# Linear attention with a mixture of experts on one core: one copy of the second layer's code per step, and evictions in one ScalarE operation

## The chip, the cores and the metric

The kernel runs on 1 core of one Trainium2 chip. The metric is the device time of the whole program in microseconds (us), the median of several runs. Engines are written as in the profile: PE is TensorE, DVE is VectorE, ACT is ScalarE, POOL is GpSimd, SP is SyncE. Each engine has its own instruction stream; a suffix q in a row (PEldq, ACTq) marks what its sequencer does: waits, branches, issues.

## What is computed

The reference is attention with positive random features, followed by a mixture of experts in which every token goes to one expert:

```python
def phi(x):                                   # x = q or k, scaled
    h = einsum('bhsd,md->bhsm', x, omega) - sum(x * x, -1, keepdims=True) / 2
    return exp(h - max(h, -1, keepdims=True)) / sqrt(m)
kv, z = einsum('bhsm,bhsd->bhmd', k_p, v), sum(k_p, axis=2)
attn = einsum('bhsm,bhmd->bhsd', q_p, kv) / (einsum('bhsm,bhm->bhs', q_p, z)[..., None] + 1e-6)

logits = x @ w_gate                           # x: 4608 tokens of 512
expert_idx = argmax(logits, axis=1)
gate_w = softmax(logits)[arange(N), expert_idx]
for e in range(8):
    mask = expert_idx == e
    out[mask] = gate_w[mask, None] * (maximum(x[mask] @ w1[e], 0) @ w2[e])
```

There are 8 batches of 8 heads with 576 positions of 64, 128 features, and 8 experts with `w1` of 512 x 1024 and `w2` of 1024 x 512. All of it is float32.

## The kernel before

The first part (class `Attention`, to about 250 us) computes the attention of all batches and writes its rows to a buffer in HBM, `token_rows`; `Routing` sorts the tokens by expert meanwhile. The second part (class `Experts`) goes over the experts in steps. A step takes up to three tiles of 128 tokens of one expert: it gathers their rows by index (POOL), turns and splits them into a high and a low part (`xh`, `xl`, on ACT and DVE), multiplies them with the expert's first layer (`l1`, L1031: three products for each pair of blocks, high by high, high by low, low by high), takes the relu into `hh` and `hl` (ACT at L1045, DVE at L1046), multiplies with the second layer (`l2`, L1072 to L1074, again three products), scales the result by the token's gate and scatters it to the output (`send` and `scatter`).

How many tokens an expert has is known only on the chip. The steps are written out in the program one after the other, and each holds the code of all its kinds: two tiles (kind 2, 256 columns in the first layer), two tiles and a half one (kind 1, 320 columns) and three tiles (kind 0, 384 columns). Each engine loads the kind into a register (L960) and branches. In `l1` this happens twice per step, once for each half of the hidden units (`part`): `If(kind > 1)` at L1059, and in its `Else` `If(kind > 0)` at L1062, so that the code of a part is, in this order, that of two tiles, of the half tile and of three tiles. The second layer is `l2(t, a)` for tile a, with 24 products of 512 columns; a half third tile has a routine of its own, `l2half`, with 16.

With this input 15 steps run, numbered here from 1: steps 4, 9 and 14 are of kind 0, steps 5, 11 and 15 of kind 1, the other nine of kind 2. From step 13 on the steps are nested in one another (`tail`), with a branch at L1166 that leaves when no step is left.

The order within an engine is that of the program. In `step`, the engines run the splits of the weights that have arrived (`change`, casts at L54 and subtractions at L48), the first layer, the gathers of step t + 2, the turning and splitting of the rows of step t + 1 (`following`), and then the second layer with its evictions and scatters. The part that the change touches is the end of `step`: `If(kind > 1)` at L1148 holds the two tiles of a two-tile step, the second of them under a flag of its own (`when`, L1111); its `Else` holds the third tile first (the branch between `l2half` and `l2(t, 2)` is at L1152) and then tiles 0 and 1 once more. Each `l2` accumulates in a PSUM bank of its own (`p_2[a]`: `p_t`, `p_snu`, `p_skv`) and ends in `send`, which evicts the bank in two halves of 256 columns: ACT takes the first (L1101), DVE the second (L1102), and POOL scatters the row tile (L1106). Both halves write one tile `y`, and DVE's half starts after ACT's.

Of the kernel before, what the change touches and what calls it, by code (L numbers as in the profile page):

```python
# [14 lines left out]
AF = mybir.ActivationFunctionType  # L15
# [6 lines left out]
DM = H * D  # L22
# [823 lines left out]
class Experts:  # L846
# [121 lines left out]
    def split(self, n, cs=range(8)):  # L968
        for c in cs:
            split_r(self.nc, *self.part(n, c), self.nc.scalar, self.nc.vector)  # L970
# [126 lines left out]
        self.send(p, self.ys[i % 3], self.gt[i % 6], idx[:, i:i + 1])  # L1097

    def send(self, p, y, gate, idx):
        c = DM // 2  # L1100
        self.nc.scalar.activation(y[:, :c], p[:, :c], AF.Copy, scale=gate)  # L1101
        self.nc.vector.tensor_scalar_mul(y[:, c:], p[:, c:], gate)  # L1102
        self.scatter(y, idx)

    def scatter(self, y, idx):
# [27 lines left out]
    def step(self, t, following, split=lambda: None):  # L1133
        engines = (ET.PE, ET.DVE, ET.Activation, ET.Pool)
        if t + 1 < NPR:
            self.flips(t + 1)
            self.flips3(t + 1)
        split()
        kind = self.kind(t, engines)
        self.l1(t, kind)  # L1140
        if t + 2 < NPR:
            self.gather(t + 2)
            self.gather3(t + 2)
        if t == 1:
            self.next(0, 2)
        following()
        self.nc.gpsimd.drain()
        with self.tc.If(kind > 1) as pair:  # L1148
            self.l2(t, 0)
            self.when(self.reg(4, t, 1, engines), lambda: self.l2(t, 1))  # L1150
        with pair.Else():
            with self.tc.If(kind > 0) as short:  # L1152
                self.l2half(t)
            with short.Else():
                self.l2(t, 2)
            for a in range(2):
                self.l2(t, a)

    def tail(self, t):
        split = lambda: self.change(t, 2)  # L1160
# [103 lines left out]
```

## Time and profile before

| what | us |
|---|---|
| median of 3 runs | 676.98 (676.61 to 679.22) |
| the profiled execution, its own time | 676.33 |
| its span, from the first to the last recorded instruction | 674.6 |
| PE busy in the span | 639.4 (95%) |
| ACT, DVE, POOL busy | 417.1, 346.1, 281.8 |
| DMA queue q8 (code) | 92 packets, 1.51 MB |

The profile records one execution. Its span is a little shorter than the time that the execution took, and the sum of a prediction is made against the latter. A row of a view that groups instructions has the line of the kernel, the engine, the operation, the tiles written and read, the shape, and a count; what stands behind the bar is the time busy, the mean of one in ns, and the idle time of the engine before them with what ended it. What ended a wait is inferred from semaphores: where the engine that is named had long been done, it was something else. Branches and register loads are not counted as busy time; they appear where one line is asked for, with shortest, median and longest duration in ns.

### The profile page before, as it was taken

Reading aid. Unit: us, or ns where it says so; the run is one execution under the profiler, and the core shown is the slowest. Engines: PE = TensorE matmul, PEld = TensorE weight load, DVE = VectorE, ACT = ScalarE, POOL = GpSimd, SP = SyncE. Lnnn points to the kernel's source line nnn. Section 1 sums busy time; section 2 is a strip of 40 time slices with the busy share of each in tenths; the row PEclk is TensorE's granted clock in tenths of the full one; section 3 lists DMA queues with packets and bytes.
Section 4 is the critical chain, followed back from the end, with each engine's and each line's share of the span. In section 5 each row is a group of like instructions: output and inputs, shape, how many; then the busy total and the mean of one; then the engine's idle time right before and its main releaser. Section 6 shows DMA issues by size and latency. Waiting matters only on the chain. (4 is left out here: it accounts for less than half of the span.)

```text
span 674.6 us, 19384 instructions
## 1 busy us (share of the span) xinstructions
PE 639.4 (95%) x7185; PEld 578.5 (86%) x7185; DVE 346.1 (51%) x825; ACT 417.1 (62%) x1040; POOL 281.8 (42%) x499
## 2 busy tenths in 40 slices
PE   6898999999998989999999999999999999999995
PEld 5788989889898977789988989988989879989884
DVE  3367979879888879932223155123245255222220
ACT  6999999999999988543334166234256265243320
POOL 8566666676767852433330302412203303312111
PEclk9999999999999999999999999999999999999998
DMA  8865474646635242475741209653219509752001
GB/s 214 227 200 144 143 213 139 188 137 182 191 112 199 89 155 68 141 253 131 147 100 27 80 3 271 176 99 67 74 61 233 182 3 262 204 84 50 35 18 39
DMA packets 113247, 90.01 MB, mean 133 GB/s; under 512 B 72126, under 2 KB 96702, under 8 KB 113088
## 3 DMA queue, kind: packets, MB, share of 16 engines
q1 hardware_dynamic: 105360, 68.78, 38.6%
q0 software_dynamic: 7184, 19.04, 8.4%
q8 instruction: 92, 1.51, 1.0%
q14 instruction: 67, 0.55, 0.3%
q10 hardware_dynamic: 544, 0.13, 0.1%
HBM read 63.46 MB, written 19.15 MB: 122 GB/s over the span
## 5 line engine op out<-in xcount | busy, mean ns | idle before, releaser
L1031 PE MATMUL p<-xh,w1p 128*128 128x256 f32 (+2 forms) x960 | 148.0, 296 | 1.8 <-DVE hh L1046 1.3
L1031 PEld LDWEIGHTS p<-xh,w1p 128*128 128x128 f32 x960 | 135.0, 188 | 4.2 <-issue 2.8
L1045 ACT ACTIVATE hh<-p 128x512 fp32r<-128x512 f32 (+2 forms) x84 | 43.6, 522 | 132.4 <-PE p L1031 126.5
L1046 DVE SCALAR_TENSOR_TENSOR hl<-p,hh 128x512 fp32r<-128x512 f32 (+2 forms) x84 | 48.2, 577 | 122.6 <-ACT hh L1045 108.4
L1106 POOL DMA_INDIRECT out_dram<-ys,idx x32 | 36.2, 1131 | 165.1 <-DVE ys L1102 58.3
L233 ACT ACTIVATE qp<-pp,mx 128x128 f32<-128x128 f32 x256 | 95.4, 723 | 0.0
L233 ACT ACTIVATE kp<-pp,mx 128x128 f32<-128x128 f32 x256 | 93.0, 681 | 0.4 <-DVE mx L221 0.2
L221 DVE TENSOR_REDUCE mx<-pp 128x8 f32<-128x1024 f32 x64 | 78.0, 1219 | 26.0 <-PE pp L214 25.6
L1031 PE MATMUL p<-xl,w1p 128*128 128x256 f32 (+2 forms) x480 | 83.3, 295 | 0.0
L192 ACT COPY tq<-tt 128x1024 f32<-128x1024 f32 x59 | 82.1, 1391 | 0.9 <-PE tt L150 0.9
L214 PE MATMUL pp<-om_t,tq 64*128 64x128 f32 x1024 | 74.5, 284 | 2.6 <-ACT qp L233 1.7
L1031 PEld LDWEIGHTS p<-xl,w1p 128*128 128x128 f32 x480 | 70.4, 188 | 0.0
L249 POOL TENSOR_TENSOR k<-kp 128x256 f32<-128x256 f32 x64 | 46.6, 728 | 55.0 <-ACT kp L233 51.4
L214 PEld LDWEIGHTS pp<-om_t,tq 64*128 64x128 f32 x1024 | 62.3, 187 | 6.3 <-ACT qp L233 3.3
L1005 ACT COPY xw<-xt 128x1024 uint16<-128x1024 uint16 x36 | 48.6, 1351 | 5.0 <-DMA xt<-xg 4.0
L1106 POOL DMA_INDIRECT out_dram<-y,idx x6 | 5.9, 990 | 106.2 <-DVE y L1102 56.1
L48 DVE TENSOR_TENSOR xl<-xw,xh 128x512 fp32r<-128x512 f32 x36 | 24.9, 692 | 46.3 <-ACT xh L54 36.6
L305 PE MATMUL nu<-kva,tq 128*64 128x73 f32 x992 | 42.3, 230 | 6.0 <-ACT kva L292 6.0
L1101 ACT ACTIVATE ys<-p_snu,gt 128x256 f32<-128x256 f32 x16 | 7.6, 475 | 64.4 <-PE p_snu L1074 49.4
L1074 PE MATMUL p_t<-w2p,hl 128*128 128x512 f32 x120 | 47.0, 392 | 0.0
L1074 PE MATMUL p_snu<-w2p,hl 128*128 128x512 f32 x120 | 47.0, 391 | 0.0
L1072 PE MATMUL p_snu<-w2p,hh 128*128 128x512 f32 x120 | 47.0, 391 | 0.0
(406 smaller groups left out, 1359.4 us busy)
## 6 DMA issues: line engine op xcount, KB each, us to landing
w1s<-in_moe_w_dram SPq DMA_DIRECT2D x5, 2048.0 KB
w2s<-in_moe_w_dram SPq DMA_DIRECT2D x5, 2048.0 KB, 11.0
v<-in_v_dram SPq DMA_DIRECT2D x32, 256.0 KB, 3.9
token_rows<-xc SPq DMA_DIRECT2D x8, 1024.0 KB
k<-in_k_dram SPq DMA_DIRECT2D x31, 256.0 KB, 4.7
q<-in_q_dram SPq DMA_DIRECT2D x31, 256.0 KB, 5.5
kr<-in_k_dram SPq DMA_DIRECT2D x16, 64.0 KB, 4.9
vz<-in_v_dram SPq DMA_DIRECT2D x16, 64.0 KB, 3.4
```

The lines of the kernel that those rows point to most:

```text
L192: self.nc.scalar.copy(self.pack(i, j), tt)
L214: nc.tensor.matmul(pp[:, a, n, i, :], th[r, k].rearrange("p a t -> p (a t)"), self.om[r, :], start=True, stop=True)
L221: nc.vector.tensor_reduce(out=mx[:, :, n], in_=s[("pp", h)][:, :, n], axis=AX.X, op=ALU.max, negate=True)
L233: nc.scalar.activation(x[:, j, :], pp[:, j % 2, n, j // 2, :], AF.Exp, bias=mx[:, j % 2, n, j // 2:j // 2 + 1])
L249: add = lambda o, x, y: nc.gpsimd.tensor_tensor(out=o, in0=x, in1=y, op=ALU.add)
L305: nc.tensor.matmul(o[r, j, :], qt[:, j, g], kva[:, a, :], start=True, stop=True)
L1005: self.nc.scalar.copy(x.bitcast(U16).rearrange("p c (t k) -> p k c t", k=2), xt.rearrange("p (k c) t -> p k c t", k=2))
L1031: self.nc.tensor.matmul(o, w[:, i, c], x[:, i, :], start=k == 0, stop=k == len(ops) - 1)
L1045: self.nc.scalar.activation(a[:, :, :n], o[:, :, :n], AF.Relu)
L1046: low = lambda d, c: self.nc.vector.scalar_tensor_tensor(out=d, in0=o[:, :, c], scalar=0.0, in1=a[:, :, c].bitcast(F32), op0=ALU.max, op1= ...
L1072: nc.tensor.matmul(p, h, self.w2h[:, c, :], start=c == 0, stop=False)
L1074: nc.tensor.matmul(p, l, self.w2h[:, c, :], start=False, stop=c == self.NF - 1)
```

## The change

Tiles 0 and 1 of the second layer stand once, after a branch that holds the third tile (or its half) alone. Steps of kind 2 skip that branch; all kinds then run `l2(t, 0)`, and `l2(t, 1)` under its flag. And `send` evicts a bank with one ACT operation of 512 columns instead of two halves on ACT and DVE.

```diff
     def send(self, p, y, gate, idx):
-        c = DM // 2
-        self.nc.scalar.activation(y[:, :c], p[:, :c], AF.Copy, scale=gate)
-        self.nc.vector.tensor_scalar_mul(y[:, c:], p[:, c:], gate)
+        self.nc.scalar.activation(y, p, AF.Copy, scale=gate)
         self.scatter(y, idx)
@@ step
         following()
         self.nc.gpsimd.drain()
-        with self.tc.If(kind > 1) as pair:
-            self.l2(t, 0)
-            self.when(self.reg(4, t, 1, engines), lambda: self.l2(t, 1))
-        with pair.Else():
+        with self.tc.If(kind < 2):
             with self.tc.If(kind > 0) as short:
                 self.l2half(t)
             with short.Else():
                 self.l2(t, 2)
-            for a in range(2):
-                self.l2(t, a)
+        self.l2(t, 0)
+        self.when(self.reg(4, t, 1, engines), lambda: self.l2(t, 1))
```

Lines of the changed kernel behind `send` are smaller by two: the branch around the third tile is at L1146, the one between its two forms at L1147, the flag of tile 1 at L1109, the eviction at L1100.

Where this moves PE's instructions, in the first step: the kernel before, from the end of the first layer into the second. After the branch at L1148 the products of tile 0 (bank `p_t`) follow at once (`w2p_5980` and `w2p_5981` are the high and the low part of the weights).

```order
L1062 UNCONDITIONAL_BRANCH
L1021 UNCONDITIONAL_BRANCH
L1111 UNCONDITIONAL_BRANCH
L1148 COMPARE_AND_BRANCH
L1072 MATMUL p_t_5896<-w2p_5980,hh 128x512
L1073 MATMUL p_t_5896<-w2p_5981,hh 128x512
L1074 MATMUL p_t_5896<-w2p_5980,hl 128x512
```

These rows of tile 0 are the first copy of two; in the changed kernel they come 44 rows further down, as the same place shows there. Behind the branch at L1146 now stands the third tile (bank `p_skv`), and a two-tile step jumps over it from there.

```order
L1062 UNCONDITIONAL_BRANCH
L1021 UNCONDITIONAL_BRANCH
L1109 UNCONDITIONAL_BRANCH
L1146 COMPARE_AND_BRANCH
L1147 COMPARE_AND_BRANCH
L1087 MATMUL p_skv<-w2p_5980,hh 128x512
L1089 MATMUL p_skv<-w2p_5981,hh 64x512
L1086 MATMUL p_skv<-w2p_5981,hh 64x512
```

The third tile's code has moved from behind the two tiles to ahead of them. PE at the end of tile 1 (bank `p_snu`), before the change: here a two-tile step jumped over the third tile and over the other kinds' copy of tiles 0 and 1.

```order
L1074 MATMUL p_snu<-w2p_5980,hl 128x512
L1111 UNCONDITIONAL_BRANCH x2
L1152 COMPARE_AND_BRANCH
L1087 MATMUL p_skv<-w2p_5980,hh 128x512
L1089 MATMUL p_skv<-w2p_5981,hh 64x512
```

The rows from L1152 on are the ones that stand ahead now, and the copy behind them is gone. After the change the next step's kind is loaded there, and its first layer (L1059) follows with no code to jump over.

```order
L1074 MATMUL p_snu<-w2p_5980,hl 128x512
L1109 UNCONDITIONAL_BRANCH x3
L960 TENSOR_LOAD flags
L960 ISA x2
L1059 COMPARE_AND_BRANCH
```

The jump at a two-tile step's end has so moved to L1146, ahead of its second layer.

## Rows read from the trace of the kernel before

**Rows 1.** Stretches: first and expert part; us, busy by engine (count), PEclk, DMA, GB/s

```profile
0.00:255.00 255.00, 230.96 (x4773) 216.68 (x4774) 195.78 (x507) 243.70 (x760) 174.07 (x361) 1.00 0.58 170
290.00:671.00 381.00, 373.81 (x2183) 336.20 (x2181) 119.80 (x223) 150.20 (x236) 94.31 (x127) 1.00 0.43 112
```

**Rows 2.** PE's waits, 285 to 675 us: us in total, times, longest

```profile
PE p L1031 <- DVE hh L1046: 1.3, 1, 1.3
PE p_skv L1087 <- DVE hh L1046: 1.2, 1, 1.2
PE p L1031 <- issue: 0.5, 1, 0.5
```

**Rows 3.** Stretches: step 5, then step 11, from first product to the next step's

```profile
378.67:407.41 28.74, 28.74 (x162) 25.67 (x161) 12.30 (x29) 13.78 (x24) 5.53 (x8) 1.00 0.18 56
528.52:560.37 31.85, 29.27 (x161) 25.70 (x160) 12.30 (x29) 13.76 (x24) 6.58 (x9) 1.00 0.28 84
```

**Rows 4.** Branches of PE's sequencer, by line, each in a window holding it alone

```profile
L1062 PEldq COMPARE_BRANCH  x1: 3311/3311/3311, 341.5 to 341.5; - x1
...
L1062 PEldq COMPARE_BRANCH  x1: 2538/2538/2538, 470.7 to 470.7; - x1
...
L1148 PEldq COMPARE_BRANCH  x1: 2792/2792/2792, 542.6 to 542.6; - x1
...
L1111 PEldq COMPARE_BRANCH  x1: 281/281/281, 340.1 to 340.1; - x1
...
L1111 PEldq COMPARE_BRANCH  x1: 297/297/297, 469.4 to 469.4; - x1
...
L1111 PEldq COMPARE_BRANCH  x1: 188/188/188, 318.2 to 318.2; - x1
...
L1059 PEldq COMPARE_BRANCH  x1: 389/389/389, 416.3 to 416.3; - x1
```

**Rows 5.** q8 packets, MB, share: 0:255, 290:668, 542.3:545.6, 416.3:421.5 (none in 416.3:420.4)

```profile
q8 instruction: 37, 0.61, 1.0%
...
q8 instruction: 51, 0.84, 1.0%
...
q8 instruction: 1, 0.02, 1.8%
...
q8 instruction: 1, 0.02, 1.1%
```

**Rows 6.** Timeline of PE: start, length, what, idle before it

```profile
322.25 0.96 PE L1031 MATMUL p<-xh,w1p 128*128 128x256 f32 x7
...
344.82 0.97 PE L1031 MATMUL p<-xh,w1p 128*128 128x384 f32 x4 [0.47 <-issue]
...
418.30 0.39 PE L1072 MATMUL p_t<-w2p,hh 128*128 128x512 f32 x1
```

**Rows 7.** Evictions: L1101 (shortest/median/longest ns), then relus by shape, 380 to 675 us

```profile
L1101 ACT ACTIVATE ys<-p_snu,gt x16: 474/474/477, 271.9 to 667.0; 128x256 f32<-128x256 f32 x16
L1101 ACT ACTIVATE ys<-p_t,gt x16: 474/475/476, 278.7 to 661.4; 128x256 f32<-128x256 f32 x16
L1101 ACT ACTIVATE y<-p_skv,gt x3: 467/474/475, 369.3 to 628.9; 128x256 f32<-128x256 f32 x3
...
L1045 ACT ACTIVATE hh<-p 128x512 fp32r<-128x512 f32 x24 | 14.1, 596 | 39.1 <-PE p L1031 39.1
...
L1045 ACT ACTIVATE hh<-p 128x384 fp32r<-128x384 f32 x16 | 7.9, 492 | 25.4 <-PE p L1031 25.4
```

**Rows 8.** Timeline of the end, all engines, after PE's last product

```profile
667.03 0.47 ACT L1101 ACTIVATE ys<-p_snu,gt 128x256 f32<-128x256 f32 x1 [5.15 <-PEq L1166]
667.54 0.48 DVE L1102 TENSOR_SCALAR ys<-p_snu,gt 128x256 f32<-128x256 f32 x1 [5.14 <-ACT ys L1101]
668.30 0.97 POOL L1106 DMA_INDIRECT out_dram<-ys,idx x1 [4.62 <-POOLq L1148]
```

**Rows 9.** Stretch in which the weights of the expert of step 6 are loaded

```profile
404.00:424.00 20.00, 20.00 (x137) 18.39 (x136) 10.26 (x17) 11.87 (x19) 6.90 (x8) 1.00 0.90 275
```

## The prediction

> **What bounds the kernel now.** I read the stages first, then the waits of TensorE (PE), then its branches. [...] PE's waits are three, of 1.3, 1.2 and 0.5 us [rows 2]. The first two lie in step 11. Steps 5 and 11 do the same work (64 rows in the third tile), yet take 28.74 and 31.85 us: 3.1 us more, nearly all of it idle PE [rows 3]. The waits view names DVE; but a branch on PE's queue lasted 2.79 us there, and two other branches lasted 3.31 and 2.54 us, where the rows beside them show 0.19 to 0.39 us [rows 4].
>
> What are these long branches? Queue q8 carries code. From 0 to 255 us, in code that never branches, it moves 37 packets while PE executes 4773 products and 4774 weight loads [rows 1, 5]: 9547/37 = 258 instructions per packet, an estimate, rounded to 256 below. In the expert part 51 packets go by for only about 4364 executed instructions [rows 1, 5]: code that is jumped over is fetched too, one piece after the other. The 2.79 us branch had exactly one such packet inside its wait [rows 5]. The long branches come where jumps follow each other closely: 340.1 and 341.5, 469.4 and 470.7 [rows 4]. My reading: a jump into the next piece is quick, because that piece is there; it also orders the piece after it, and a second jump that already needs this one waits for it. From the first jump to the end of the wait it took 341.5 + 3.31 - 340.1 = 4.7 us, and 470.7 + 2.54 - 469.4 = 3.8 us [rows 4].
>
> PE itself stands only if this outlasts what is queued ahead of it. That cover depends on the place. At the end of a step's second layer, the jump at 318.2 is issued 4.05 us before PE takes up the next first layer at 322.25; at the end of a first layer, the jump at 416.3 is issued only 2.0 us before the second layer starts at 418.30 [rows 4, 6]. So the 4.7 us wait left PE idle for 0.47 us (0.64 more between two starts than usual) before 344.82 [rows 6], and the 3.8 us one left nothing.
>
> **The change, part by part.**
>
> *Evictions.* Each of the 35 evictions in 256-column halves takes 0.475 us on ACT, then 0.48 on DVE [rows 7, 8]; now it is one ACT operation of 512. Relu evictions of 384 and 512 columns take 492 and 596 ns [rows 7], 104 ns for 128 columns, so 256 more cost 208: 0.68 us. Bounds: 0.60 (the 512-column relu) and 0.95 us (two halves); the value taken is nearest the lower row, which reads the same memory. In 34 of the 35 places PE's products hide it: the bank is used again a step later, and ACT gains only 35 x 0.21 = 7 us beside 230 idle [rows 1]. What stands behind an eviction on ACT is at most the next weight casts, whose results PE needs only a first layer later. At the end it is exposed: ACT starts at 667.03, DVE ends at 668.02, POOL's scatter starts at 668.30 [rows 8]. 0.99 us become 0.68: **-0.3 us** (from -0.4 to 0).
>
> *The flag in steps with a third tile.* These six steps gain a flag load and a branch between tiles 0 and 1, on every engine. Two-tile steps have them now, and PE's waits show no gap for them [rows 2], with about 4 us of products queued. Nothing, as long as that queue stands; without it, some 0.5 us per step.
>
> *The jump that moves.* A two-tile step falls straight into its second layer and jumps over the rest after it, under 4.05 us of cover. Now it jumps ahead of it, right behind the jump that ends the first layer, under 2.0 us. Counted in the built program (a matmul is two instructions), the two skip 197 and 89: 286 in a row, more than a piece of 256. Where the first starts less than 30 instructions ahead of a piece's edge, both cross an edge, and the second must wait. One place of the edges, at remainder about 190 of 256 in that count, explains all three long branches. In the changed program a step is about 97 instructions shorter, 783 instead of 880, which is 3 pieces and 15, so the place drifts slowly: the first jump starts at remainder 167 in step 6, 182 in step 7 and 197 in step 8. In 6 and 7 both jumps cross; in 8 the edge lies 7 instructions before the first jump, which is nearly the same. In 10 and 12 (remainders 227 and 1) it lies 37 and 67 before: mostly over. In 1, 2, 3 and 13 the second edge comes late enough.
>
> The price of one is the wait less the cover. The quick case is 3.8 - 2.0 = 1.8 us, the slow one 4.7 - 2.0 = 2.7. In step 6 weights are being loaded, DMA is 0.90 busy from 404 to 424 [rows 9], and the packet ordered at 416.3 had not begun by 420.4: its window shows one only when drawn out to 421.5 [rows 5]. With at most the 2.8 us of a whole wait behind that, PE would start about 422.9 instead of 418.30: 4.6 us. I take 4.6 for step 6, 2.4 for step 7, 1.8 for step 8, and 0.4 each for 10 and 12: **+9.6 us**. Bounds: 1.8 for the first three alone, 5.4 us; 4.6 for each of these with 1.5 for the others, 16.8 us.
>
> [...]
>
> *Stalls that go.* With the edges elsewhere, step 4 loses its 0.64 us, since the jump at 340.1 is gone, and step 11 its 3.1 us: its jumps now cross edges over 7 us apart, a half of its first layer. **-3.7 us** (to 0, should the new places be as bad).
>
> **Sum:** 9.6 - 3.7 - 0.3 = +5.6 us on the profiled execution's 676.33, whose span is 674.6 with 1.7 around it: 681.9. That execution lies 0.65 under the median of the runs, 676.98, so a measured 682.6.
>
> **Rivals.** *No new stall.* If PE's queue holds enough code ahead, or the piece after next is ordered early, the two jumps cost some 0.5 us of issue under 2.0 us of cover, and the old stalls go with their places: 676.98 - 3.7 - 0.3 = 673.0, faster by 0.6%. It decides from the point where the wait from the first jump is under 2.0 us. For it: PE stands for code in only two of fifteen steps now. Against it: the three long branches were jumps of only about 100 instructions each. [...]
>
> *Stalls at the quick price.* If the packets of steps 6 to 8 come as the one after 469.4 did, it is 1.8 + 1.8 + 1.4 + 0.4 = 5.4 us, less 4.0: 678.4, no difference that can be told. For it: the loads move with the steps and may have passed. Against it: the packet after 416.3.
>
> *Dearer.* An ACT or DVE that meets such a wait in a first layer with a third tile, where a bank is used again after two groups of 12 products, would add some 2 us: 685. Their code shifts too; no wait of PE on them shows before, once step 11 is explained [rows 2].
>
> **How the numbers follow.** A measurement of this kernel can tell about 0.5%, 3.4 us, from no change: 673.6 and 680.4 bound it. My forecast has 0.45 and the dearer case 0.10, nearly all of it slower; the quick price has 0.25, no new stall 0.20. Some of the last would keep a part of step 11's stall and end within 0.5%, and some of the quick price ends above 680.4. That makes faster 0.15, same 0.27, slower 0.58. The range reaches from 674.5, into the rival without stalls, to 687.5, a slow price in two more places; both signs are in it. The forecast's own range is 679.5 to 687.
>
> **What would show it.** In the changed profile: branches at L1146 on PE's queue of 3 to 6 us in steps 6, 7 and 8, each with a q8 packet in it and PE idle 1.5 to 5 us before L1072; steps 5 and 11 equally long; no gap before step 4; fewer q8 packets in the expert part, about 15 x 783/256 = 46; ACT evictions of 0.6 to 0.75 us, and the last scatter 0.3 us nearer to PE's last product. I am wrong if L1146 stays under 0.5 us throughout, or if PE's idle time sits elsewhere.

## The result and the profile after

The changed kernel takes 690.06 us in the median of 6 runs (683.68 to 698.45), the kernel before 676.8 beside it. The ratio goes by the four runs of the fast state, whose median is 686.11, and leaves out the two longest, 695.45 and 698.45, as slow: 1.0149 times as long, 95% interval 1.0104 to 1.0193, about 10 us (9.3 by these medians). The profiled execution took 692.69 us, span 691.0: 16.4 more than the profiled one of before, and 6.6 above that median. Where do the 16.4 us lie?

The expert part, 290 us to the last product at 684.50, and PE's waits from 290 us on:

```profile
290.00:684.50 394.50, 382.17 (x2189) 342.33 (x2187) 104.16 (x191) 156.75 (x235) 93.58 (x125) 0.98 0.41 106
```

```profile
PE p_t L1072 <- PEq L1146: 11.2, 5, 4.1
PE p L1031 <- issue: 0.5, 1, 0.5
```

PE was busy 98% of this part before, at a granted clock of 1.00 [rows 1], so what lets PE stand or slows it sets the time; now it stands 12 us, and the granted clock is 0.98. The waits view puts all but 0.5 us down to PE's own sequencer at L1146, the branch that now stands between the layers. DVE, which the waits of before named [rows 2], is gone from them. The branches, each in a window holding it alone; these are steps 6, 7, 8 and 10, the last row is the end of step 12's first layer:

```profile
L1146 PEldq COMPARE_BRANCH  x1: 5573/5573/5573, 418.1 to 418.1; - x1
...
L1146 PEldq COMPARE_BRANCH  x1: 3978/3978/3978, 446.1 to 446.1; - x1
...
L1146 PEldq COMPARE_BRANCH  x1: 2810/2810/2810, 472.1 to 472.1; - x1
...
L1146 PEldq COMPARE_BRANCH  x1: 2061/2061/2061, 528.6 to 528.6; - x1
...
L1059 PEldq COMPARE_BRANCH  x1: 5242/5242/5242, 580.3 to 580.3; - x1
```

They answer to the three long branches of [rows 4], and there are more of them, under less cover. In step 12 the branch at L1146 takes 0.23 us: the long one ahead of its second layer is the one at L1059. Code packets from 290 us to the last product, where there were 51 [rows 5]; and, from 418 to 424 us, the one inside the 5.57 us branch:

```profile
q8 instruction: 45, 0.74, 0.7%
...
q8 instruction: 1, 0.02, 1.0%
```

In all five the last packet ends 1.4 to 1.5 us before the branch does; the one in step 6 starts only 3.1 us after its branch, the one in step 7 1.6 us. What such a branch leaves of PE shows in its timeline, in steps 6, 7, 8 and 12 (start, length, and in brackets the idle time before it):

```profile
423.94 0.57 PE L1072 MATMUL p_t<-w2p,hh 128*128 128x512 f32 x1 [4.14 <-PEq L1146]
424.31 0.63 PE L1073 MATMUL p_t<-w2p,hh 128*128 128x512 f32 x1
424.73 0.63 PE L1074 MATMUL p_t<-w2p,hl 128*128 128x512 f32 x1
...
450.27 0.47 PE L1072 MATMUL p_t<-w2p,hh 128*128 128x512 f32 x1 [2.24 <-PEq L1146]
...
475.04 0.47 PE L1072 MATMUL p_t<-w2p,hh 128*128 128x512 f32 x1 [1.05 <-PEq L1146]
...
586.04 0.77 PE L1072 MATMUL p_t<-w2p,hh 128*128 128x512 f32 x1 [3.50 <-PEq L1146]
```

There is a second loss here. Behind the gap before 423.94 the next products start 0.42 us apart, where the same products were 0.23 apart before: the second product of step 6's second layer there (the first is in [rows 6]), and the start of step 7:

```profile
418.53 0.40 PE L1073 MATMUL p_t<-w2p,hh 128*128 128x512 f32 x1
...
429.25 1.11 PE L1031 MATMUL p<-xh,w1p 128*128 128x256 f32 x8
```

The granted clock of stretches behind the four gaps, the column behind the counts:

```profile
423.94:427.94 4.00, 4.00 (x11) 3.18 (x12) 0.70 (x1) 0.23 (x1) 0.99 (x3) 0.57 0.60 209
450.27:455.27 5.00, 5.00 (x15) 3.98 (x16) 1.39 (x2) 2.14 (x3) 0.00 (x0) 0.66 0.24 56
475.04:479.04 4.00, 4.00 (x18) 3.30 (x19) 1.59 (x3) 3.94 (x5) 0.00 (x0) 1.00 0.09 20
586.04:591.80 5.76, 5.76 (x14) 4.53 (x15) 0.69 (x1) 0.88 (x2) 1.48 (x4) 0.53 0.82 250
```

Behind the idle times of 4.1, 2.2 and 3.5 us the granted clock is 0.57, 0.66 and 0.53 on the mean of these stretches; behind the one of 1.05 us it stays at 1.00. From 427.94 to 436.00 us and from 454.92 to 460.00 it is 1.00 again. By the first products of each layer, step 6's second layer takes 436.56 - 423.94 = 12.6 us against 429.25 - 418.30 = 10.95 before, step 7's 12.66 against 11.01, step 12's 13.5 against 10.9: 5.9 us together.

Steps 5 and 11, and step 2, in which PE waits for no code:

```profile
380.00:408.74 28.74, 28.74 (x162) 25.68 (x161) 11.33 (x27) 14.21 (x24) 5.52 (x8) 1.00 0.17 53
541.86:570.55 28.69, 28.69 (x161) 25.68 (x160) 11.33 (x27) 14.20 (x24) 5.63 (x9) 1.00 0.21 64
...
301.65:323.93 22.28, 22.13 (x145) 19.99 (x144) 4.15 (x6) 7.51 (x10) 7.15 (x9) 1.00 0.61 133
```

Step 11 has lost its 3.1 us [rows 3]. Step 2 took 322.25 - 300.36 = 21.89 us before and takes 0.39 more. There, PE's branch, a semaphore instruction, and the second layer's first weight load:

```profile
L1146 PEldq COMPARE_BRANCH  x1: 233/233/233, 310.9 to 310.9; - x1
L1146 PEldq EVENT_SEMAPHORE  x1: 51/51/51, 312.8 to 312.8; - x1
...
312.84 0.19 PEld L1072 LDWEIGHTS p_t<-w2p,hh 128*128 128x128 f32 x1 [0.32 <-issue]
```

The branch is over in 0.23 us, but the semaphore instruction goes through only at 312.8, when PE's first-layer products are through (the last ends at 312.72), and the load follows it. The view of L1146 has this instruction nine times, as often as there are two-tile steps. My reading: the products in the skipped branch count up a semaphore, and the path that skips them has an instruction of its own for that count. It goes through 0.04 us behind PE's last queued product in each of steps 1, 2, 3 and 13. These steps are about 0.4 us longer than before.

The end:

```profile
684.68 0.69 ACT L1100 ACTIVATE ys<-p_snu,gt 128x512 f32<-128x512 f32 x1 [4.95 <-PEq L1161]
685.64 0.98 POOL L1104 DMA_INDIRECT out_dram<-ys,idx  x1 [4.63 <-ACT ys L1100]
```

The scatter starts 685.64 - 684.50 = 1.14 us behind PE's last product, 1.43 before [rows 8; last product 666.87].

| profiled execution, us | forecast | measured |
|---|---|---|
| new idle PE, steps 6, 7, 8, 10, 12 | 4.6, 2.4, 1.8, 0.4, 0.4 = 9.6 | 4.1, 2.2, 1.05, 0.3, 0.5 + 3.5 = 11.7 |
| lower clock behind it | 0 | 5.9 |
| semaphore on the skip path | 0 | 1.6 |
| stalls that go, steps 4 and 11 | -3.7 | -3.8 |
| eviction at the end | -0.3 | -0.3 |
| sum | 5.6 | 15.1 |

Of the 1.3 us to 16.4, PE's first step began 0.9 later (279.02 against 278.12), the end behind the scatter's start is 1.0 shorter, and the first layers ahead of the gaps are 0.2 us longer than the gap explains, in step 12, with two gaps, 0.6.

Step 12 alone is 7.2 us longer than before in this execution (29.01 against 21.81 us). That is about as much as this execution lies above the median of 686.11. Experiment 2, in which step 12 loses 0.9 us, takes 686.27. Whether the other executions of the changed kernel lack step 12's wait was not seen.

### The profile page after: what moved, and what is told of

Read it like the earlier page. It is cut to its first block, busy times and chain, and to the rows that moved or that the text cites. A ratio compares the mean times of both kernels' runs of the same rounds, so it can differ in the third digit from the quotient of the medians.

```text
span 691.0 us, 19381 instructions
## 1 busy us (share of the span) xinstructions
PE 649.0 (94%) x7185; PEld 585.9 (85%) x7185; DVE 328.8 (48%) x790; ACT 424.0 (61%) x1040; POOL 282.4 (41%) x499
## 5 line engine op out<-in xcount | busy, mean ns | idle before, releaser
L1104 POOL DMA_INDIRECT out_dram<-ys,idx x32 | 33.4, 1042 | 179.8 <-ACT ys L1100 93.7
L233 ACT ACTIVATE qp<-pp,mx 128x128 f32<-128x128 f32 x256 | 93.9, 702 | 0.0
L233 ACT ACTIVATE kp<-pp,mx 128x128 f32<-128x128 f32 x256 | 91.6, 661 | 0.5 <-POOL kz L242 0.3
L1072 PE MATMUL p_t<-w2p,hh 128*128 128x512 f32 x120 | 50.0, 417 | 11.8 <-PEq L1146 11.2
L1100 ACT ACTIVATE ys<-p_snu,gt 128x512 f32<-128x512 f32 x16 | 11.0, 688 | 66.6 <-PE p_snu L1074 53.6
L1074 PE MATMUL p_t<-w2p,hl 128*128 128x512 f32 x120 | 49.3, 411 | 0.0
L1073 PE MATMUL p_t<-w2p,hh 128*128 128x512 f32 x120 | 49.2, 410 | 0.0
```

Of the source, the lines that this page charges most:

```text
L233: nc.scalar.activation(x[:, j, :], pp[:, j % 2, n, j // 2, :], AF.Exp, bias=mx[:, j % 2, n, j // 2:j // 2 + 1])
L1072: nc.tensor.matmul(p, h, self.w2h[:, c, :], start=c == 0, stop=False)
L1073: nc.tensor.matmul(p, h, self.w2l[:, c, :], start=False, stop=False)
L1074: nc.tensor.matmul(p, l, self.w2h[:, c, :], start=False, stop=c == self.NF - 1)
```

## The experiments

**1. The evictions alone.** The kernel before with

```diff
-        self.nc.scalar.activation(y[:, :c], p[:, :c], AF.Copy, scale=gate)
-        self.nc.vector.tensor_scalar_mul(y[:, c:], p[:, c:], gate)
+        self.nc.scalar.activation(y, p, AF.Copy, scale=gate)
```

> The kernel before with nothing changed but the evictions (one ACT operation of 512 columns). Theory (the loss comes from code waits at the moved jump): 676.8 - 0.3 = 676.5 us, no difference that can be told; PE's idle time stays where it was, before the first layer of step 4 and in step 11; the last scatter starts 0.2 to 0.4 us nearer to PE's last product. Rival (the wider evictions hold up PE or ACT): most of the changed kernel's 10 to 13 us appear here, 685 us or more, with PE waiting for ACT in the second layers.

675.18 us, ratio 0.9983 (0.9969 to 0.9996). PE's waits from 285 us on are those of before, in step 11:

```profile
PE p_skv L1087 <- DVE hh L1046: 1.5, 1, 1.5
PE p L1031 <- DVE hh L1046: 1.2, 1, 1.2
```

The evictions cost nothing and gain 0.2%. So the loss is the branch's.

**2. The branch alone.** The changed kernel with `send` in halves again (the diff above, backwards).

> The changed kernel with the evictions in halves again (ACT 256 columns, then DVE 256). Theory: PE's code is the same, so the waits are too: branches of 3 to 6 us ahead of the second layer in steps 6, 7 and 8, 2 us in step 10, 4 to 6 us at the end of step 12's first layer, and 684 to 694 us. Rival (evictions): back to 677 to 680 us.

686.27 us, ratio 1.0147 (1.012 to 1.0173): the whole loss. Its branches ahead of the second layer last 6.8, 3.8, 2.0 and 2.4 us in steps 6, 7, 8 and 10. The one at the end of step 12's first layer lasted 1.8 us and not 5.2: the 4 to 6 us that were expected there did not come, and this wait differs between two programs whose PE code is nearly the same.

**3. The same code, 72 instructions further on.** The changed kernel with a branch ahead of step 1's first layer that is never entered:

```diff
         kind = self.kind(t, engines)
+        if t == 1:
+            with self.tc.If(self.kind(t, (ET.PE,)) < 1):
+                for _ in range(33):
+                    self.nc.tensor.transpose(self.p_x[0][:, :P], self.ident, self.ident)
         self.l1(t, kind)
```

> The changed kernel with 66 TensorE instructions that never run, in a branch ahead of step 1; with the branch itself all later code of PE lies 72 instructions further on. Nothing else of the work changes. Theory (two jumps in a row cross two edges of the code pieces): the first jumps now start at remainders 155, 179 and 194 in steps 1 to 3, and at 239, 254, 269, 299, 329 and 345 in steps 6, 7, 8, 10, 12 and 13, with the edge at 190. So the long branches ahead of the second layer move to steps 1, 2 and 3 (2 to 4 us each, more in step 1 where weights are loaded at 281 to 302 us), and steps 8, 10 and 12 lose theirs; steps 6 and 7 keep at most 1.3 us of idle PE. Time 680 to 690 us. Rival (the jump costs this wherever its code lies, or loads set the place): the idle time stays in steps 6, 7, 8 and 12, 4.1, 2.2, 1.1 and 4 us.

692.54 us, ratio 1.024 (1.0216 to 1.0264), 2.5 us above the range that was expected. Its long branches ahead of the second layer, each in a window of its own (L1153 is L1146 there):

```profile
L1153 PEldq COMPARE_BRANCH  x1: 6232/6232/6232, 287.5 to 287.5; - x1
...
L1153 PEldq COMPARE_BRANCH  x1: 4076/4076/4076, 316.9 to 316.9; - x1
...
L1153 PEldq COMPARE_BRANCH  x1: 3680/3680/3680, 341.5 to 341.5; - x1
...
L1153 PEldq COMPARE_BRANCH  x1: 5812/5812/5812, 428.7 to 428.7; - x1
```

They moved to steps 1, 2 and 3, where nothing waited; steps 7, 8, 10 and 12 are free of them. Same work, other steps: the waits belong to where the code lies. The miss is step 6, which kept 4.2 us of idle PE instead of at most 1.3, with its packet starting 3.4 us after the branch: code is late there for another reason as well (experiment 9).

**4. The third tile last.** In `step` of the changed kernel the branch stands behind tiles 0 and 1:

```diff
-        with self.tc.If(kind < 2):
-            ...
         self.l2(t, 0)
         self.when(self.reg(4, t, 1, engines), lambda: self.l2(t, 1))
+        with self.tc.If(kind < 2):
+            ...
```

> The changed kernel with the third tile's branch behind tiles 0 and 1 instead of ahead of them; the code is as long and stands once. [...] Rival (a code wait per two-tile step wherever the branch stands, or a shorter step that is itself unlucky): 680 us or more, with long branches at the third tile's line.

690.64 us, ratio 2.2% above (1.0195 to 1.0246). 672 to 674.5 us were expected, below both kernels, with PE standing for code less than 1 us in all 15 steps and the granted clock staying up: wrong, by a wait that I hadn't thought of. No branch over 1.1 us is left but the last one, yet PE stands ahead of nine first layers and once within one (waits from 278 us on, then the end of step 2: PE's semaphore instruction and its last branch, ACT's semaphore instruction, and PE's first product):

```profile
PE p L1031 <- ACTq L1148: 7.5, 6, 1.7
PE p L1031 <- ACTq L1109: 5.4, 3, 2.2
PE p L1031 <- issue: 1.4, 1, 1.4
```

```profile
L1148 PEldq EVENT_SEMAPHORE  x1: 51/51/51, 322.7 to 322.7; - x1
...
L1059 PEldq COMPARE_BRANCH  x1: 68/68/68, 323.6 to 323.6; - x1
...
L1148 ACTq EVENT_SEMAPHORE  x1: 17/17/17, 323.5 to 323.5; - x1
...
323.76 0.50 PE L1031 MATMUL p<-xh,w1p 128*128 128x256 f32 x2 [1.10 <-ACTq L1148]
```

The semaphore instruction of the skip path again, at a dearer place. PE's goes through when PE's products are through (322.7); only then does PE load the next kind and branch on it, with an empty queue, until 323.70. The first weight load follows at 323.75. The view names ACT, but ACT's instruction had gone through at 323.49, and so it is in all nine places: ACT's is 0.1 to 0.9 us earlier than the load, which starts 0.04 to 0.06 us behind the end of PE's own last branch. The wait is PE's alone.

**5. A product in place of the semaphore instruction.** The changed kernel with

```diff
-        with self.tc.If(kind < 2):
+        with self.tc.If(kind < 2) as more:
             ...
+        with more.Else():
+            self.nc.tensor.transpose(self.p_2[2][:8, :8], self.ident[:8, :8], self.ident[:8, :8])
```

> The changed kernel; where a two-tile step skips the third tile, PE now gets one product of 8 x 8 that nothing reads, in place of a semaphore instruction that waits for PE's own first-layer products. Theory: that semaphore instruction is a second cost of the change, about 0.3 us in each two-tile step that has no code wait: the gaps of 0.15 us and the late weight load ahead of the second layer in steps 1, 2, 3 and 13 go, the long branches in steps 6, 7, 8, 10 and 12 stay (their idle time is set by the branch). 1 to 3 us below the changed kernel: 684 to 689 us. Rival (the gaps are the jump's own time): they stay, and the time is the changed kernel's.

684.99 us, ratio 1.0128 (1.009 to 1.0166). The instruction is gone, the gap with it, but the 8 x 8 product takes nearly as long itself: step 2 lasts 323.20 - 300.99 = 22.21 us, 22.28 in the changed kernel. The long branches stay (6.5, 3.8, 1.5, 2.1 us). The time lies in the expected range but can't be told from the changed kernel's, so it settles nothing.

**6. The third tile between tiles 0 and 1,** with that product on the skip path.

```diff
+        self.l2(t, 0)
         with self.tc.If(kind < 2) as more:
             ...
         with more.Else():
             self.nc.tensor.transpose(self.p_2[2][:8, :8], self.ident[:8, :8], self.ident[:8, :8])
-        self.l2(t, 0)
         self.when(self.reg(4, t, 1, engines), lambda: self.l2(t, 1))
```

> As e5, with the third tile's branch between tiles 0 and 1. Theory: the jump now has tile 0's 12 products queued ahead of it, 3.4 us instead of 2.0, and no semaphore drains PE; the branches that last 2 to 4 us leave no idle PE, one of 5 to 7 us in step 6 leaves 2 to 3. The long waits of the kernel before (steps 4 and 11) are gone, since code stands elsewhere. 671.5 to 675.5 us, at or below the kernel before with the new evictions (675.2). Rival (a semaphore wait again, of ACT on its own eviction behind tile 0): PE idle of 0.5 to 1 us ahead of tile 1 in nine steps, 680 us.

674.67 us, ratio 1.0002 (0.9982 to 1.0021). (A tile has 24 products, not 12. I take the cover as about 4 us, an estimate from the 4.05 us that lay between the jump at 318.2 and the next first layer in the kernel before [rows 4, 6].) Of branches of 3.1, 1.1 and 2.8 us none leaves PE idle, and one wait of 0.5 us is left in the whole part. The longer cover explains it: under the 2.0 us of the changed kernel's place, 3.1 and 2.8 us would have left about 1 us each, an estimate from [rows 4, 6]. There are also fewer long branches here, and none over 3.1 us. But the two-tile steps still last longer than before, step 2 with no idle time at all:

```profile
301.44:323.66 22.22, 22.22 (x146) 19.92 (x145) 4.17 (x6) 7.52 (x10) 6.63 (x9) 1.00 0.65 127
```

**7. The third tile last, with the product,** and `self.p_x = [self.two[1], two]` in place of `[two, self.two[1]]`. The second edit does not do what it was meant for: the first layer writes the banks `p_1`, and `p_x` is used by the routing alone.

> As e4 (third tile last), with the 8 x 8 product on PE's skip path, and with the two banks of the first layer in the other order, so that the first group of the next step doesn't use the third tile's bank. Theory: e4's 1.2 to 2.3 us of idle PE at the start of nine steps came from two semaphore instructions of the skipped branch, PE's on its own products and ACT's on its own eviction; without the one and with the other 1.3 us away, they go, and 4 us of queued products cover the code waits: 671 to 674.5 us. Rival (the code of the longer skip costs this time by itself): 685 us or more.

675.55 us, ratio 1.0014 (0.9994 to 1.0033). Experiment 4's 15 us are gone: 690.64 - 675.55. So they were in the main PE's semaphore instruction, with the load and the branch that wait behind it, and not the place of the code. ACT's semaphore instruction is still there (at 322.5 in step 2) and stops nothing: PE's next first layer has begun by then, at 321.73. The time is 1 us above what was expected: here too step 2 takes 0.3 us more than before for the product.

**8. The count carried by work that is there anyway.** As 6, but without the 8 x 8 product: the last of tile 0's eight chunks (three products) and its eviction stand on both paths.

```diff
+        self.l2(t, 0, range(self.NF - 1))
         with self.tc.If(kind < 2) as more:
+            self.l2(t, 0, (self.NF - 1,))
             ...
         with more.Else():
-            self.nc.tensor.transpose(self.p_2[2][:8, :8], self.ident[:8, :8], self.ident[:8, :8])
+            self.l2(t, 0, (self.NF - 1,))
```

> As e6, but the skip path gets no extra product: tile 0's last chunk (three products) and its eviction stand in both paths of the branch instead, so that they carry the count. Theory: e6 paid 0.3 us in each of nine two-tile steps for the 8 x 8 product, which ate what it won in steps 4 and 11 (0.6 and 3.2 us). Without it these steps take 21.9 us again: 9 x 0.3 = 2.7 us below e6, 671.5 to 673.5, faster than the kernel before by 0.3 to 0.6%. Rival (the 0.3 us is the branch's own, or three products lie on an expensive path): as e6, 674 to 676 us.

675.35 us, ratio 0.9983 (0.9966 to 1.0001). Steps 2 and 12, then the only waits from 285 us on:

```profile
300.88:322.77 21.89, 21.89 (x146) 19.92 (x144) 4.15 (x6) 7.52 (x10) 6.79 (x9) 1.00 0.69 137
557.12:583.41 26.29, 23.97 (x145) 21.18 (x144) 8.88 (x14) 11.57 (x18) 7.03 (x9) 0.94 0.89 258
```

```profile
PE p_t L1075 <- issue: 2.0, 1, 2.0
PE p L1031 <- issue: 0.4, 1, 0.4
```

Step 2 is back at 21.89 us, as before: the 0.3 to 0.4 us was the count. But step 12 lost 4.5 us. No long branch is in it: PE stands in the middle of tile 0, with DMA 0.89 busy, until 1.5 us after a code packet has ended (568.8 to 569.8). From 571.26 its products then start 0.34 to 0.43 us apart, against 0.23 in the kernel before, and the granted clock of the step is 0.94. I read this as straight code that ran out. So the forecast of 671.5 to 673.5 failed, and the time is the rival's for another reason.

**9. No weight loads.** The changed kernel without the loads of later experts' weights:

```diff
-        (self.dma1 if n == 1 else self.dma2)(bass.ds(e, 1))
+        if t < 2:
+            (self.dma1 if n == 1 else self.dma2)(bass.ds(e, 1))
```

> The changed kernel without the weight loads of the later experts, issued in steps 6, 10 and 12 (each first layer's and second layer's 2 MB); the products go on with the first weights loaded. Theory: the loads only lengthen code waits that the double jump makes. Idle PE ahead of the second layer in step 6 falls from 4.1 to about 2.2 us, as in step 7, with no long stretch at the lower clock behind it; step 12 has at most 0.5 us; steps 7 and 8 keep 2.2 and 1.1 us. 678 to 683 us. Rival (the loads cause the waits altogether): steps 6, 7 and 8 lose theirs too, 673 to 676 us. Other rival (loads have no part): steps 6 and 12 keep 4.1 and 3.5 us, 684 us or more.

681.49 us, ratio 1.0068 (1.0046 to 1.009). Steps 6, 7 and 8, then step 12's start of the second layer:

```profile
L1147 PEldq COMPARE_BRANCH  x1: 3772/3772/3772, 418.2 to 418.2; - x1
...
L1147 PEldq COMPARE_BRANCH  x1: 3795/3795/3795, 442.8 to 442.8; - x1
...
L1147 PEldq COMPARE_BRANCH  x1: 2201/2201/2201, 468.6 to 468.6; - x1
```

```profile
577.64 0.47 PE L1072 MATMUL p_t<-w2p,hh 128*128 128x512 f32 x1 [0.22 <-PEq L1147]
```

Step 6 now waits as long as step 7, 3.8 us, with 2.2 us of idle PE in place of 4.1, and step 12 is down to 0.2. Step 7 stays, at 2.1 us of idle PE, and step 8 keeps a branch of 2.2 us with 0.4 us of idle PE. So the double jump makes the waits, and the weight loads lengthen those that fall into them. They do it by a late start: step 6's packet starts 1.4 us behind the branch here, 3.1 in the changed kernel, 4.5, 3.4 and 4.0 in experiments 2, 3 and 5, and lasts 0.9 to 1.0 us in all of them.

**10. Experiment 8 with its code 208 instructions further on,** by the never entered branch of experiment 3 with `range(101)`.

> As e8, with 202 TensorE instructions that never run ahead of step 1; with their branch all later code of PE lies 208 further on, as in e3 it lay 72. Theory: e8's one stall left, 2.0 us idle and 1.6 us at the lower clock in step 12, is a piece of straight code that was ordered while weights were loading; with the edges 208 instructions away the piece is ordered at another point, 12 no longer waits, and no other step does: 16.9 to 17.1 us for steps 4's and 14's first layers as before, no idle PE over 0.5 us anywhere, 670.5 to 673 us, faster than the kernel before by 0.5 to 0.8%. Rival (step 12's stall belongs to the loads, whatever the code's place): it stays, 674 to 676 us. Other rival: a stall of 2 to 5 us appears in step 1, where weights are also loading, 675 us or more.

673.7 us, ratio 0.9949 (0.993 to 0.9967): 0.7 us above the forecast, but 0.5% faster than the kernel before, and than the changed one by about 13 us, from the two ratios. The waits from 285 us to the last branch, and the whole expert part:

```profile
PE p_t L1078 <- issue: 0.3, 1, 0.3
```

```profile
290.00:666.20 376.20, 375.86 (x2199) 338.02 (x2197) 105.26 (x193) 157.30 (x237) 94.23 (x125) 1.00 0.43 112
```

PE stands 0.3 us in 376, behind a branch of 3.6 us in step 10. Step 12's wait is gone with the code's new place. That the place of experiment 8 gave no gain that could be told and this one 0.5% shows how much hangs on the place. From the first product of step 1 to the last, this part takes 666.21 - 280.43 = 385.8 us; 388.75 before, 405.5 in the changed kernel.

## Why the prediction was right, and where its sum was short

Slower was forecast, at 682.6 us; the ratio makes it about 687 (1.0149 x 676.98), at the upper end of the range. The median of all six runs, 690.06, lies beyond it. That the range held is in part luck: its upper end stood for a slow price in two more places, and what filled it was in the main two terms that the sum did not have, the lower clock and the semaphore, and step 12.

**The mechanism held, place by place.** Long branches at L1146 in steps 6, 7 and 8 with a code packet inside, none ahead of step 4, step 11 as long as step 5, 45 packets where 46 were forecast: all there. Only step 8's branch and idle time, 2.81 and 1.05 us, lie below the signs that the prediction gave. Experiment 3 moved the waits by moving the code alone, to the steps that the count of instructions named, except for step 6: 72 instructions brought branches of 6.2, 4.1 and 3.7 us into steps 1, 2 and 3, where L1146 lasts 0.23 to 0.24 us in the changed kernel. That bears out that the place counts. The size of a piece stays an estimate, from the 258 instructions per packet [rows 1, 5], and the place of the edges was fitted to three long branches [rows 4]; no run shows either by itself.

**The price in steps 6 and 7 was about right, step 8's too high.** 4.6, 2.4 and 1.8 us were forecast, 4.1, 2.2 and 1.05 measured. That step 6's extra 2 us come from the weight loads was argued then from one late packet; experiment 9 shows it.

**Step 12 was mis-sized: 0.4 forecast, 4.0 measured.** The term took it as "mostly over", from the place of the edge alone. But step 12 lies in a weight load like step 6 (DMA 0.85 busy from 570.55 to 599.56). PE ran dry for 0.5 us in straight code there, until 1.6 us behind a packet's end at 576.9, and the next packet started only at 583.2, so the jump at L1059 waited 5.2 us. Runs with nearly the same code had 1.8 and 1.3 us at this branch (experiments 2 and 5), and without loads 0.2 us of idle PE is left. So the loads have a part in it; why that packet came so late in this execution stays open. The bound of 1.5 us for this place was too low.

**The lower clock was missing from the sum.** The forecast priced a stall by the time that PE stands. 5.9 us more came behind them, as much as the whole forecast. Nothing in the profile of before had to show it: its longest wait on PE in this part was 1.3 us [rows 2], at a granted clock of 1.00 [rows 1].

**The semaphore on the skip path was missing too.** The jump's term priced its code wait alone, so steps 1, 2, 3 and 13 stood at nothing. In the kernel before, a two-tile step took a side of this branch that holds products; the new branch has an empty side, and a two-tile step takes that one. It was 0.4 us in each of four steps here, and most of the 15 us in experiment 4. In steps with a code wait it hides behind the branch: in step 6 it goes through at 423.8, 0.1 us behind the branch's end. The flag between tiles 0 and 1, costed at nothing, did cost nothing: step 5 lasts 28.74 us as before.

**The evictions** took 0.688 us for 0.68 forecast, and the end moved by the 0.3 us. The whole was worth 0.2% (experiment 1), a little more than that: step 4's stall of 0.64 us was also gone there.

**The rivals.** No new stall, and stalls at the quick price, fell: the branch of 5.57 us at L1146 left PE idle for 4.1. Dearer, with ACT or DVE waiting for code, didn't happen: no wait of PE on them is left. The time came out near that rival's 685, for other reasons.

## What to carry to other kernels

Count the instructions that a jump skips, and those of the jumps close ahead of it: where they together passed a piece of code here (197 and 89 instructions against about 258 a packet, an estimate), PE waited for a transfer, 2.8 to 5.6 us in steps 6, 7 and 8, and what was queued ahead of the jump was all that hid it: 1.4 to 1.8 us, the branches less the idle times behind them. Put a skipped block where the queue is fullest (in experiment 6 branches of 3.1 and 2.8 us left no idle PE), and let both sides of the branch end in work that is there anyway, so that no instruction has to wait just to keep the counts equal (step 2 took 22.28 us with that wait in the changed kernel, 21.89 without it in experiment 8). Allow for a stall of PE to cost more than its length: 1.4 to 1.75 times in steps 6, 7 and 12 here, though some stalls of 2.0 to 2.4 us in experiments 3 and 9 cost their length alone. Look at what loads run while the code is fetched: without them step 6's idle time fell from 4.1 to 2.2 us (experiment 9). And where a view says that an engine waits for another, look whether that other had long been done (experiment 4).

## What was not expected of the hardware

PE's waits for code end about the same time behind the end of a packet: 1.4 to 1.5 us in the five branches of the changed kernel, with packets of 0.9 to 1.2 us, and as much in experiment 9 without the loads. The branch of 3.31 us ahead of step 4 in the kernel before ended 2.0 us behind one. What varies most is when the packet starts.

Behind every idle time of PE of 3.5 us or more in the expert parts of these runs the granted clock fell, on the mean of the 4 to 6 us behind it: to 0.57 and 0.53 behind 4.1 and 3.5 us in the changed kernel, to 0.71 behind 5.4 us in experiment 2, to 0.50 and 0.52 behind 5.1 and 4.2 us in experiment 3 and to 0.67 behind 5.0 us in experiment 5. Behind idle times of 2.0 to 2.4 us it fell in step 7 of the changed kernel (0.66), of experiments 2 and 5 (0.66 from 449.25 to 454.25 and from 450.25 to 455.20) and of experiment 9 (0.67 from 446.77 to 452.00), and in step 12 of experiment 8 (0.94 over the whole step), but not in steps 2 and 3 of experiment 3 (1.00 from 321.18 to 325.18 and from 345.33 to 349.33), nor in step 6 of experiment 9 (1.00 from 422.19 to 427.20). What tells these apart stays open. And the changed kernel's times spread more, 683.68 to 698.45 us, against 675.35 to 679.84 beside it. Waiting for code alone does not explain that: the four runs of experiment 3 lie within 1.4 us.
